# Attention in 64-key blocks on array tiles, even and odd tokens apart: one tuned kernel, one change of plan

## The chip, the cores and the metric

One core of one Trainium2 chip runs the whole program. The metric is the time on the device in microseconds (us); the median of several runs is quoted, with the lowest and highest. The engines are called PE (TensorE's matmuls), PEld (TensorE's weight loads, which overlap the matmuls), DVE (VectorE), ACT (ScalarE), POOL (GpSimd) and SP (SyncE, which issues transfers).

A *tile* below is one step of the attention: 112 query rows with the 16 rows of keys before them. A *row tile* is 128 rows of the residual stream, as the gMLP layers use it. The *tail* of a tile is everything after the attention proper: transpose o, multiply by `wo`, add the residual, normalise for the next layer.

## The reference, cut to what matters

There are four layers, attention, gMLP, attention, gMLP, each `x + f(layernorm(x))`, on 2048 tokens of 576 channels. The gMLP layers take about three quarters of the time and are untouched by the change. The attention has 32 heads of 18 channels; a token looks at 8 tokens, itself and every second one before it:

```python
W, dil = (8, 2)
off = jnp.arange(W) * dil
idx = pos[:, None] - off[None, :]          # tokens s, s-2, ..., s-14
...
logits = jnp.einsum('bhsd,bhswd->bhsw', q, kg) * scale
attn = _softmax(logits, axis=-1)
o = jnp.einsum('bhsw,bhswd->bhsd', attn, vg)
return o.transpose(...).reshape(B, S, D) @ wo
```

An even token sees only even tokens, an odd one only odd ones. A dense 128 x 112 block of logits, masked, is therefore at least half wasted, and the change goes after that.

## The kernel before: the parts that matter here

A tile is done in two half steps of 16 heads. Per half step there are 16 logits matmuls, one or two exponentials, one mask, 16 value products and one normalisation. o is transposed by a transfer on SP's queue. Filler matmuls (`JUNK`, two per half step, 128 rows x 512 columns, never read) run in the late steps.

```python
def JUNK(n):
    ...
        jt = self.PT_tile([P, 512], f32, "junk")
        for k_ in range(n):
            nc.tensor.matmul(jt[:, :], lhsT=wo_sb[:, k_ % 4, 0:P], rhs=wo_sb[:, (k_ + 1) % 4, 0:512],
                             start=True, stop=True)
...
def TAIL_A(t):                                   # half steps after the tile's last: 2
        nc.sync.dma_start_transpose(out=oT_t[:, :, :nq], in_=o_t[:nq, :])
        ...
def TAIL_B(t):                                   # 4: output product, residual, statistics
        ...
def TAIL_B2(t):                                  # 5: normalise, on POOL
        st["xn"] = self.ln_xn(x_new, st["nq"], mv, rstd, nmr, eng="pool")
...
ND0 = 3                                          # 3 of 5 channel groups projected before the first logits
...
for (off, fn) in ((2, TAIL_A(t)), (4, TAIL_B(t)), (5, TAIL_B2(t)), (6, TAIL_C(t))):
    s_ = plast + off
```

The normalisation is on POOL.

The softmax here doesn't subtract the row's maximum and nothing guards it: scores larger than these inputs give would overflow.

## Time and profile before

Before: 1348.4 us median (1346.5 to 1352.3, 4 runs beside the changed kernel; 1349.1 in the three first runs).

| stretch (profiled run) | us | how read |
|---|---|---|
| attention, layer 1 | 162.9 (25.2 to 188.1) | first projection matmul to first gMLP matmul |
| gMLP | 501.1 (188.1 to 689.2) | to the first projection of layer 2 |
| attention, layer 2 | 159.4 (689.2 to 848.6) | |
| gMLP and end | 499.8 (848.6 to 1348.4) | |
| first projection to first value product | 29.3 and 26.7 | layers 1 and 2 |
| late tile | 5.8 | value products of one tile to those of the next |

The head of the page: the second line gives each engine's busy time, share of the span and number of instructions; PEclk is TensorE's granted clock in tenths, over 40 equal slices.

```profile
span 1348.4 us, 21451 instructions
...
PE 1249.9 (93%) x8656; PEld 659.5 (49%) x8656; DVE 616.5 (46%) x1402; ACT 384.2 (28%) x595; POOL 356.4 (26%) x487
...
PEclk9999989999999999997999999899999999999999
```

The averages say nothing about the attention, which is a quarter of the span. The window table does. Columns: window, its length, then busy us and instruction count of each engine, the granted clock, the DMA engines' share, GB/s. These are the late steps of layer 1, and most of layer 2:

```profile
112.00:145.00 33.00, 30.22 (x497) 20.50 (x496) 29.63 (x74) 24.06 (x34) 20.88 (x14) 1.00 0.81 125
145.00:178.00 33.00, 29.48 (x498) 19.74 (x496) 29.75 (x77) 19.27 (x30) 18.29 (x13) 1.00 0.66 121
740.00:836.00 96.00, 87.93 (x1377) 57.37 (x1376) 81.70 (x196) 62.12 (x85) 53.02 (x36) 0.98 0.74 143
```

DVE is busy 29.7 of 33 us in the late steps and PE nearly as much, at full clock. In the timeline of one late tile (start, length, engine, line, operation):

```profile
808.18 1.19 SPq L568 DMA_TRANSPOSE oT_7002<-o_t_6993  x1
808.26 0.56 POOL L164 TENSOR_TENSOR ln_rstd<-ln_rstd,neg_half 112x1 f32<-112x1 f32 x1 [2.85 <-DVE ln_rstd L163]
808.92 2.29 POOL L181 TENSOR_SCALAR ln_xn_82<-x_new,ln_mv,ln_rstd 112x576 bf16<-112x576 f32 x1
...
809.50 1.40 PE L582 MATMUL pw<-wo_sb,oT_7004 128*128 128x288 bf16 x10
...
811.11 0.59 PE L517 MATMUL junk<-wo_sb 128*128 128x512 bf16 x2 [0.21 <-DVE v_ext L375]
```

The normalisation takes 2.29 us.

### The profile page before, as it was taken

How to read it: one execution, taken by the hardware profiler on the slowest of the kernel's cores; microseconds unless marked ns; L12 is line 12 of the kernel's file. 1: busy time of each engine (PE TensorE's matmuls, PEld its weight loads, DVE VectorE, ACT ScalarE, POOL GpSimd, SP SyncE). 2: the span in 40 equal slices, each digit the busy share in tenths (PEclk: the TensorE clock that was granted, in tenths of full speed). 3: DMA queues.
4: the chain of work that ended last, by engine and by line, in shares of the span. 5: the costliest groups of instructions: out<-in, count | busy, mean ns of one | idle time of the engine just before them, and what ended most of it. 6: DMA issues, size and time to landing. Idle time of an engine off the chain costs nothing.

```text
span 1348.4 us, 21451 instructions
## 1 busy us (share of the span) xinstructions
PE 1249.9 (93%) x8656; PEld 659.5 (49%) x8656; DVE 616.5 (46%) x1402; ACT 384.2 (28%) x595; POOL 356.4 (26%) x487
## 2 busy tenths in 40 slices
PE   1999969989999999998998987899999999999997
PEld 0456644434444444445754655444444444444576
DVE  4468858843322332332534878588323223333221
ACT  2556726620011111001126665465101111100000
POOL 7445547830000000002141646488000000000111
PEclk9999989999999999997999999899999999999999
DMA  9449759020000000009653677861100000000232
GB/s 264 98 94 145 121 134 214 1 90 6 9 10 9 10 9 9 0 4 266 179 137 62 151 145 129 181 125 41 43 9 9 10 9 9 2 7 1 72 113 67
DMA packets 180128, 101.04 MB, mean 75 GB/s; under 512 B 138276, under 2 KB 162212, under 8 KB 180028
## 3 DMA queue, kind: packets, MB, share of 16 engines
q1 hardware_dynamic: 170208, 84.15, 28.1%
q10 hardware_dynamic: 6364, 8.55, 2.2%
q0 software_dynamic: 3456, 6.96, 2.2%
q8 instruction: 68, 1.11, 0.3%
q14 instruction: 32, 0.26, 0.1%
HBM read 41.16 MB, written 16.52 MB: 43 GB/s over the span
## 4 chain that ended last, share of the span: by engine, by line
PE 62%; DVE 11%; POOL 10%; issue 7%; DMA 6%; ACT 3%; SPq 1%; ACTq 0%; POOLq 0%; DVEq 0%
PE pg L904 36%; PE po L941 9%; DVE z_junkD L819 4%; PE pp L412 3%; DMA QK<-stg 2%; POOL ln_xn_84 L181 2%; POOL ln_xn_81 L181 1%; POOL ln_rstd L164 1%; POOL z_rstd L835 1%; POOL ln_xn_83 L181 1%; POOL ln_xn_82 L181 1%; DMA wout_b<-in_B_w_out_dram 1%; DMA wv_sb<-in_A_wqkv_dram 1%; DMA win2b<-in_B_w_in_dram 1%; DVE z_msq L828 1%
## 5 line engine op out<-in xcount | busy, mean ns | idle before, releaser
L908 DVE TENSOR_TENSOR g_tmp<-pg,bsp 128x512 f32<-128x512 f32 x144 | 99.4, 692 | 435.5 <-PE pg L904 423.9
L412 PE MATMUL pp<-xnT,wqk_sb 128*128 128x512 bf16 x400 | 100.7, 394 | 29.8 <-DMA xnT<-ln_xn_84 28.5
L812 PEld LDWEIGHTS <-xnT 128*128 128x128 bf16 x800 | 78.4, 98 | 97.0 <-issue 13.0
L812 PE MATMUL pz<-win2a,xnT 128*128 128x512 bf16 x384 | 103.1, 379 | 5.9 <-ACT zp L816 4.4
L164 POOL TENSOR_TENSOR ln_rstd<-ln_rstd,neg_half 112x1 f32<-112x1 f32 (+2 forms) x70 | 43.4, 621 | 152.3 <-DVE ln_rstd L163 152.1
L812 PE MATMUL pz<-win2b,xnT 128*128 128x512 bf16 x256 | 77.0, 386 | 6.9 <-DMA win2b<-in_B_w_in_dram 6.9
L816 ACT ACTIVATE zp<-pz 128x1024 bf16<-128x1024 f32 x64 | 65.0, 1020 | 44.6 <-POOL z2b_9746 L845 18.9
L412 PEld LDWEIGHTS <-wqk_sb 128*128 128x128 bf16 x400 | 36.9, 100 | 71.2 <-issue 36.0
L819 DVE CUSTOM_DVE_ANT_0 z_junkD<-zp 128x1536 bf16<-128x1536 bf16 x32 | 56.9, 1777 | 18.7 <-ACT zp L816 18.7
L370 PE MATMUL pv<-wv_sb,xnT 128*128 128x288 bf16 (+1 forms) x380 | 62.2, 286 | 0.2 <-DVE stg L418 0.2
L76 POOL DMA_DIRECT2D wout_b<-in_B_w_out_dram x14 | 7.5, 541 | 172.4 <-PE pg L904 172.4
L76 POOL DMA_DIRECT2D QK<-stg x52 | 31.5, 608 | 73.0 <-ACT stg L420 28.0
L584 DVE TENSOR_TENSOR x_new<-pw,xo 112x288 f32<-112x288 f32 (+1 forms) x76 | 33.5, 445 | 18.0 <-PE pw L582 10.7
L420 ACT CAST stg<-pp 128x512 bf16<-128x512 f32 x54 | 31.0, 585 | 37.4 <-PE pp L412 22.7
L370 PEld LDWEIGHTS <-xnT 128*128 128x128 bf16 (+1 forms) x380 | 33.5, 97 | 15.8 <-issue 1.4
L489 PE MATMUL L_ps<-QK 18*128 18x112 bf16 (+1 forms) x1216 | 32.0, 210 | 4.9 <-DMA QK<-stg 1.7
L418 DVE CAST stg<-pp 128x512 bf16<-128x512 f32 x26 | 18.0, 691 | 37.0 <-PE pp L412 33.5
L159 DVE BATCH_NORM_STATS2 ln_st<-x_new 112x6 f32<-112x288 f32 (+1 forms) x76 | 33.9, 449 | 1.2
L489 PEld LDWEIGHTS <-QK 18*128 18x128 bf16 (+1 forms) x1216 | 20.4, 93 | 25.6 <-issue 21.6
L845 POOL TENSOR_SCALAR z2b_3101<-zp,z_rstd,z_nmr 128x256 bf16<-128x256 bf16 x16 | 32.4, 2024 | 0.0
L845 POOL TENSOR_SCALAR z2b_9746<-zp,z_rstd,z_nmr 128x256 bf16<-128x256 bf16 x16 | 32.4, 2023 | 0.0
L904 PE MATMUL pg<-W_sb,z2b_3093 128*128 128x512 bf16 x128 | 28.4, 379 | 1.9 <-DVE z2b_3093 L848 1.9
(549 smaller groups left out, 2513.3 us busy)
## 6 DMA issues: line engine op xcount, KB each, us to landing
xres_73<-x_new SPq DMA_DIRECT2D x18, 252.0 KB
xo<-xres_74 SPq DMA_DIRECT2D x18, 252.0 KB
xres_75<-x_new SPq DMA_DIRECT2D x18, 252.0 KB
QK<-stg POOLq DMA_DIRECT2D x52, 72.0 KB, 3.8
win2a<-in_B_w_in_dram SPq DMA_DIRECT2D x2, 1728.0 KB
QK<-stg SPq DMA_DIRECT2D x48, 72.0 KB
wqk_sb<-in_A_wqkv_dram ACTq DMA_DIRECT2D x4, 576.0 KB
out_dram<-ob SPq DMA_DIRECT2D x16, 144.0 KB
```

The source lines that it names most:

```text
L164: nc.gpsimd.tensor_tensor(out=rstd[:nrows, :], in0=rstd[:nrows, :], in1=self.neg_half[:nrows, :], op=ALU.pow)
L181: e.tensor_scalar(out=xn[:nrows, 0:D], in0=x_t[:nrows, :], scalar1=mv[:nrows, 0:1], scalar2=rstd[:nrows, 0:1], op0=ALU.subtract, op1=ALU.mult)
L370: nc.tensor.matmul(pv[:nk, 0:288], lhsT=self.xnT[:, c, QT * t:QT * t + nk], rhs=wv_sb[:, c, hh * 288:(hh + 1) * 288], start=(c == 0), stop ...
L412: nc.tensor.matmul(pp[:, :], lhsT=wqk_sb[:, c, wc0:wc0 + P], rhs=self.xnT[:, c, col0:col0 + 512], start=(c == 0), stop=(c == 4))
L489: nc.tensor.matmul(L_ps[:nk, j, ftl * QT:ftl * QT + nq], lhsT=kT[32 * j:32 * j + DH, g, QT * t:QT * t + nk], rhs=qT[32 * j:32 * j + DH, g, ...
L812: nc.tensor.matmul(pzvs[ci][:, sub * 512:sub * 512 + w], lhsT=self.xnT[:, c, PADL + i * P:PADL + (i + 1) * P], rhs=win2(c)[:, c0 + sub * 5 ...
L816: nc.scalar.activation(out=zp[:, c0:c0 + cn], in_=pzvs[ci][:, 0:cn], func=ACT.Gelu_apprx_tanh, accum_out=sums[:, ci:ci + 1])
L819: nc.vector.tensor_tensor_reduce(out=junkD[:], in0=zp[:, 0:SQ_D], in1=zp[:, 0:SQ_D], scale=1.0, scalar=0.0, op0=ALU.mult, op1=ALU.add, acc ...
L845: nc.gpsimd.tensor_scalar(out=z2b[b][:, i, :], in0=zp[:, b * 256:(b + 1) * 256], scalar1=rstd[:, 0:1], scalar2=nmr[:, 0:1], op0=ALU.mult, ...
L904: nc.tensor.matmul(pg[:, :], lhsT=z2b[jj][:, i, sub * P:(sub + 1) * P], rhs=W_sb[:, i, q * 512:(q + 1) * 512], start=(i == 0), stop=(i == ...
L908: nc.vector.tensor_tensor(out=tmp[:], in0=pg[:, :], in1=bsp[:, q * 512:(q + 1) * 512], op=ALU.add)
L941: nc.tensor.matmul(acc[hh], lhsT=uT[j // 2][:, j % 2, i * P:(i + 1) * P], rhs=wout_j(j)[:, hh * 288:(hh + 1) * 288], start=(j == 0), stop= ...
```

## The change

The intent is to relieve DVE. Even and odd tokens are kept apart (`QK[..., r, ...]`), so a tile needs two 64-key by 56-query blocks a head instead of one of 128 by 112: half the logits to exponentiate and mask. The blocks go to tiles of the PE array, two column halves for even and odd. All 32 heads are done in one step. o is transposed by TensorE against a permutation (which also puts the rows back in order). Tails work on 128 rows, 16 instead of 19 of them. Core of the diff:

```diff
-        def L_mm(s):                                  # 16 per half step
-                nc.tensor.matmul(L_ps[:nk, j, ftl * QT:ftl * QT + nq], lhsT=kT[...], rhs=qT[...],
-                                 start=True, stop=True, tile_position=(32 * j, 0))
+        def L_mm(t):                                  # 64 per tile
+                            nc.tensor.matmul(L_ps[64 * r:64 * r + nk, j, g * QH:g * QH + nq],
+                                             lhsT=QK[rows, g, 2 + r, k0:k0 + nk],
+                                             rhs=QK[rows, g, r, k0 + PADL // 2:k0 + PADL // 2 + nq],
+                                             start=True, stop=True, tile_position=(32 * j, 64 * r))
...
-        def JUNK(n):                                  # filler: gone
...
+        def OT(t):
+                tp = self.H_tile("tp")                # 12 matmuls against self.perm
+                nc.scalar.copy(out=oT[...], in_=tp[...])
...
-                nc.sync.dma_start_transpose(out=oT_t[:, :, :nq], in_=o_t[:nq, :])
...
-                st["xn"] = self.ln_xn(x_new, st["nq"], mv, rstd, nmr, eng="pool")
+                st["xn"] = self.ln_xn(x_new, P, mv, rstd, nmr, eng="act")
...
-        for d in range(ND0):                          # 3 of 5 groups, then logits
-            for cc in cb_ccs(0):
+        for cc in range(2):                           # all 5 groups, all heads
+            for d in range(ND):
+                pro.append((4 * cc + 3, PG(d, cc)))
...
-            for (off, fn) in ((2, TAIL_A(t)), (4, TAIL_B(t)), (5, TAIL_B2(t)), (6, TAIL_C(t))):
+            post.append((t + 2, 0, OT(t)))
+            post += [(t + 1, 3, TAIL_A(u)), (t + 2, 1, TAIL_B(u)), (t + 3, 2, TAIL_B2(u)), (t + 3, 4, TAIL_C(u))]
```

V, projections, value products, transposed o and output product (`pv`, `pp`, `O_ps`, `tp`, `pw`) now all take turns in two PSUM buffers (`H_tile`), where the kernel before had three small ones and one for the value products.

## The prediction

> **What bounds the kernel now.** By the window table, the 1348 us span holds two attention layers (0 to 188 us, 689 to 851 us); the rest are gMLP layers (PE about 97% busy), which the change leaves alone.
>
> - Prologue: 60 q/k projection matmuls before the first logits (46.5 and 704 us in the tile view of L_ps).
> - Early steps, with the other 140 projection matmuls: PE-bound (30.2 of 32 us in 80:112, 29.2 of 30 us in 740:770).
> - Late steps: a 112-row tile takes about 5.8 us (the chain of waits repeats so). DVE is fullest, 59.4 of 66 us in 112:178. Per tile it runs two masks of 1.09 us, two reciprocals of 0.25, two normalisations of 0.46, two residual adds and two statistics of 0.45. PE has slack: junk matmuls fill it, and the timeline shows it waiting for DVE.
>
> **What the change removes and adds, per tile.**
>
> DVE: even and odd tokens apart halve the masked logits, so one mask replaces two; reciprocal, normalisation and residual add are merged; 16 tails replace 19. My sum falls from 5.9 to about 3.9 us. POOL's 2.29 us normalisations go to ACT (0.87 us). ACT: exponentials halve from 3.7 to 1.84 us, but v and oT copies and the normalisation bring it back to about 4.1 us. Neither should bind.
>
> PE: the trace gives start-to-start 12 to 13 ns for a four-row-tile logits matmul, 25 ns for a value product, 122 ns for N=288. Before: logits 0.66 us with mode switches, PV 0.8, V 1.23, output 1.23, junk 0.86: 4.8 us. After: logits and value products double in number, 32 to 64 each, on 64-column tiles. The Trainium skill (TensorEngine Tiling (Array Packing), Tile-to-Partition Mapping, Restrictions) says column tiling disables Fast Weight Load; and (Tiling Modes, Key Properties) that changing mode drains TensorE, which shows here as about 0.1 us. I estimate 13 ns a matmul with four tiles in flight: logits 0.85, PV 0.85, V 1.25, oT 0.5, output 1.23, more switches 0.6: about 5.3 us. So the late bound moves from DVE (5.8) to PE (5.3 to 5.8).
>
> The prologue needs all 100 first-half projection matmuls (216 ns each) before the first logits: 8.6 us later, work taken out of the early steps. In the second attention layer this start is exposed, with the QK transfers behind it; in the first it overlaps the layernorm ramp. The tail loses its transpose DMA (PE waits 4 us for it at 178.7 us): about -3 us a layer.
>
> **Sum.** First attention layer about -10 us, second about -5 us. Tuned orders usually recover a little more: **1332 us**, range 1290 to 1368. Faster by over 2%: 0.38; within 2%: 0.46; slower: 0.16.
>
> **What would show it right or wrong.** First logits near 50 and 715 us; the gMLP stretch unchanged (about 501 us); late tile period 5.0 to 5.8 us, PE fullest, DVE near 65%; logits and PV about 0.9 us each per tile in the timeline; no oT wait before the gMLP layer.
>
> **What would make it wrong.** First, the small-tile rate. At 7 ns a matmul the tile costs 4.5 us and the kernel about 1310; at 25 ns (weight loads of column tiles not overlapping) PE costs 6.8 us a tile and the kernel about 1380. Second, V, projections, PV, oT and output now share two PSUM buffers (before, three plus one), so PE may wait for ACT's in-order queue; it would show as PE waits released by ACT copies of v_ext, stg or oT. Third, the QK transfers, two thirds on POOL's queue, may delay the first logits.

## The result, and the profile after

After: 1433.9 us median (1430.2 to 1437.3, 4 runs), against 1348.4. Ratio 1.063 (95% interval 1.059 to 1.067): slower by over 6%. (A ratio here is the mean time of one kernel's runs over the mean of the other's of the same rounds, so not quite the ratio of the medians quoted.) The result is correct.

| stretch (profiled runs) | before | after | difference |
|---|---|---|---|
| attention, layer 1 | 162.9 | 207.1 | +44.2 |
| gMLP | 501.1 | 500.0 | -1.1 |
| attention, layer 2 | 159.4 | 197.7 | +38.3 |
| gMLP and end | 499.8 | 500.7 | +0.9 |
| first projection to first value product | 29.3, 26.7 | 46.5, 42.9 | +17.2, +16.2 |
| late tile | 5.8 | 7.8 to 9.2 | |

The loss is in the attention layers alone. It is not in the late tiles alone: by the first value products of tiles 0, 9 and 18, of the 44.2 and 38.3 us the start takes 17.2 and 16.2, the next nine tiles, with projections among them, 17.0 and 9.7, and the last nine 10.7 and 13.1. (7.8 to 9.2 us is the usual length of a late tile; one step a layer has no output product, and around it and at the layer's end they are shorter.) The page's head after:

```profile
span 1431.1 us, 27266 instructions
...
PE 1292.7 (90%) x11735; PEld 699.0 (49%) x11840; DVE 557.9 (39%) x1198; ACT 368.7 (26%) x563; POOL 292.5 (20%) x462
...
PEclk9988767999999999998999976599999999999998
```

Two things are visible. DVE, ACT and POOL all became *less* busy, as intended, and the span is longer. And PEclk dips to 5, 6 and 7 exactly in the slices of the attention. Windows of the late tiles of both layers:

```profile
135.00:165.00 30.00, 25.62 (x642) 17.59 (x639) 12.04 (x25) 13.07 (x18) 6.20 (x11) 0.66 0.30 73
165.00:195.00 30.00, 23.56 (x616) 17.38 (x616) 13.39 (x27) 14.67 (x20) 4.68 (x6) 0.76 0.24 64
870.00:900.00 30.00, 24.17 (x591) 16.85 (x591) 12.00 (x25) 12.96 (x17) 5.88 (x8) 0.66 0.31 88
```

Neither DVE, ACT nor POOL is half busy. PE is busy for 79 to 85% of the time, but at two thirds to three quarters of the clock. So nothing is full at full clock, and the tile takes half as long again. This suggests a ring: a chain of work in which each step waits for the one before, and which closes on itself. The chain of waits (start, length, what) shows one:

```profile
878.69 1.04 POOL ln_rstd L177
...
879.82 0.27 POOL ln_nmr L181
...
880.12 0.87 ACT ln_xn L190
880.99 0.61 ACT oT L484
...
881.64 3.07 PE pw L505 x12
...
884.74 0.77 DVE x_new L507
...
885.53 0.82 DVE ln_st L172 x2
...
886.68 0.72 DVE o_t L467
...
887.61 1.33 POOL ln_rstd L177
...
889.33 0.87 ACT ln_xn L190
890.19 0.61 ACT oT L484
...
890.85 3.08 PE pw L505 x12
```

From one `pw` to the next are 9.21 us. The output product of row tile u feeds DVE's residual and statistics (with the attention's own `o_t` between them in DVE's queue), then POOL's reciprocal root, then ACT's normalisation `ln_xn`. Behind `ln_xn`, in ACT's queue, stands the copy of oT. That copy has nothing to do with `ln_xn`: its own input, the transposing product, was done at 889.12 us, and yet the copy started at 890.19, when `ln_xn` ended. The next output product needs the copy. So row tile u + 1 cannot start its output product until row tile u has been normalised. Nothing in the mathematics asks for this. Nor can it be read off the code: there `OT` of step t + 3 is emitted before `TAIL_B2` of the same step, and the trace has them the other way round.

In the groups of instructions, the last columns are the idle time before the group and what ended most of it:

```profile
L505 PE MATMUL pw<-wo_sb,oT 96*128 96x288 bf16 x384 | 77.0, 371 | 36.2 <-ACT oT L484 36.2
L438 ACT ACTIVATE P_sb<-L_ps 128x896 bf16<-128x896 f32 (+1 forms) x76 | 63.7, 887 | 88.4 <-PE O_ps L458 78.6
```

PE waited 36.2 us for ACT's copy; ACT in turn waited 78.6 us for PE's value products, which stand behind `pw` in PE's queue and must be done before a P buffer is written again. The two queues hold each other up. Also, `pw` takes 3.07 us at a granted clock of 0.50 (window 881.7 to 884.6 us); the same twelve matmuls take 1.64 us at full clock. So the 9.21 us are not the ring alone. TensorE was busy for 7.5 us of them, much of that because its clock was low, and waited 1.73 us.

### The profile page after: what moved, and what is told of

It is laid out like the page before. It is cut to its first block, busy times and chain, and to the rows that moved or that the text cites. A ratio compares the mean times of both kernels' runs of the same rounds, so it can differ in the third digit from the quotient of the medians.

```text
span 1431.1 us, 27266 instructions
## 1 busy us (share of the span) xinstructions
PE 1292.7 (90%) x11735; PEld 699.0 (49%) x11840; DVE 557.9 (39%) x1198; ACT 368.7 (26%) x563; POOL 292.5 (20%) x462
## 5 line engine op out<-in xcount | busy, mean ns | idle before, releaser
L803 PE MATMUL pg<-W_sb,z2b 128*128 128x512 bf16 x2254 | 501.0, 379 | 4.5 <-DVE z2b L747 1.9
L803 PEld LDWEIGHTS <-z2b 128*128 128x128 bf16 x2304 | 225.3, 98 | 273.7 <-DVE z2b L747 2.4
L798 ACT ACTIVATE z1T<-pz 128x1024 bf16<-128x1024 f32 x72 | 73.7, 1023 | 556.8 <-PE pz L795 526.6
L795 PE MATMUL pz<-xnT,w 128*128 128x512 bf16 x710 | 163.3, 382 | 3.7 <-DMA w<-in_B_w_in_dram 3.2
L840 PEld LDWEIGHTS <-uT 128*128 128x128 bf16 x1152 | 114.3, 99 | 44.1 <-issue 12.0
L840 PE MATMUL po<-wout_b,uT 128*128 128x288 bf16 x864 | 116.0, 291 | 10.6 <-DMA wout_b<-in_B_w_out_dram 10.5
L795 PEld LDWEIGHTS <-w 128*128 128x128 bf16 x720 | 70.5, 98 | 90.6 <-DMA w<-in_B_w_in_dram 5.1
L505 PE MATMUL pw<-wo_sb,oT 96*128 96x288 bf16 x384 | 77.0, 371 | 36.2 <-ACT oT L484 36.2
L808 DVE TENSOR_TENSOR uT<-g_tmp,z1T 128x512 bf16<-128x512 f32 x144 | 99.5, 692 | 16.0 <-ACT z1T L798 6.0
L744 POOL TENSOR_SCALAR z2b<-zp,z_rstd,z_nmr 128x256 bf16<-128x256 bf16 x96 | 102.4, 1076 | 3.9 <-POOL z_nmr L736 0.9
L438 ACT ACTIVATE P_sb<-L_ps 128x896 bf16<-128x896 f32 (+1 forms) x76 | 63.7, 887 | 88.4 <-PE O_ps L458 78.6
```

Of the source, the lines that this page charges most:

```text
L505: nc.tensor.matmul(pw[:, hh, 0:288], lhsT=oT[:, c, P * u:P * u + P], rhs=wo_sb[0:96, c, hh * 288:(hh + 1) * 288], start=(c == 0), stop=(c ...
L744: nc.gpsimd.tensor_scalar(out=z2b[b][:, i, :], in0=zp[:, b * 256:(b + 1) * 256], scalar1=rstd[:, 0:1], scalar2=nmr[:, 0:1], op0=ALU.mult, ...
L795: nc.tensor.matmul(pz1[:, qq, :], lhsT=w1[:, c, sub * P:(sub + 1) * P], rhs=self.xnT[:, c, PADL + (q2 + qq) * 512:PADL + (q2 + qq + 1) * 512],
L798: nc.scalar.activation(out=z1T[:, q2 * 512:(q2 + nq2) * 512], in_=pz1[:, 0:nq2, :].rearrange("p a b -> p (a b)"), func=ACT.Gelu_apprx_tanh)
L803: nc.tensor.matmul(pg[:, :], lhsT=z2b[jj][:, i, sub * P:(sub + 1) * P], rhs=W_sb[:, i, q * 512:(q + 1) * 512], start=(i == 0), stop=(i == ...
L808: nc.vector.tensor_tensor(out=u[:, sub, q * 512:(q + 1) * 512], in0=tmp[:], in1=z1T[:, q * 512:(q + 1) * 512], op=ALU.mult)
```

## The experiments

Three theories, not exclusive, were on the table:

- **O**, the order of ACT's queue makes the ring.
- **C**, the clock: dropping the filler let TensorE's clock fall, and everything else follows from that.
- **P or Q**, the start: the first value product comes 17 us later in each layer, because of the projections' staging buffers (P) or of the transfers of QK (Q).

All ratios are to the kernel before, of the same rounds. The rounds ran on four chips; the median of the kernel before was 1347.3 to 1349.2 us in all of them, so plain times of different rounds compare to within a few us. The expectations use the letters a little differently: "theory Q" in x2, x3 and x4 is O here, and so is "rival R" in y2; "rival S" is that column-tiled matmuls are too slow.

### x1_stg5: a fifth staging buffer

```diff
-        NVB = 6
+        NVB = 4
-  stg_tiles[(d, cb)] = sb.tile([P, 4, CBW // 2], bf16, name="stg", tag="stg", bufs=4)
+  stg_tiles[(d, cb)] = sb.tile([P, 4, CBW // 2], bf16, name="stg", tag="stg", bufs=5)
```

(Two V buffers were given up to make room.)

> The changed kernel with five staging tiles for the projections in place of four (and four v tiles in place of six, to make room). Theory P: in the prologue five head groups are open at once but only four staging tiles exist, so the fifth group's copy out of PSUM waits for a QK transfer and holds one of the two PSUM buffers; PE then runs the second five groups single-buffered (3.5 us a group in place of 2.2). Expected: first value product of the second attention layer 6 to 10 us earlier after its first projection (43 us now), 12 to 20 us off the whole kernel, about 1417 us. Rival (QK transfers set the start): nothing changes, within 4 us of 1434.

Measured: 1433.8 us (1431.8 to 1434.9), ratio 1.064, unchanged. In layer 2 fifty projections ran back to back in 10.96 us, and yet the first value product came 43.2 us after the first projection (42.9 in the changed kernel). In the table of waits (total, times, longest) the logits now wait 16.7 us for the transfers, where they waited 3.5 us in the changed kernel (first line):

```profile
PE L_ps L427 <- DMA QK<-stg: 3.5, 4, 1.5
PE L_ps L427 <- DMA QK<-stg: 16.7, 13, 3.6
```

Theory P falls: faster projections only moved the wait to the transfers. This leaves the transfers, when they can begin and how long their queues need; y3 tests it.

### x2_xn_after_exp: normalise behind the next exponentials

```diff
-  (t + 3, 2, TAIL_B2(u)), (t + 3, 4, TAIL_C(u))
+  (t + 5, 2, TAIL_B2(u)), (t + 5, 4, TAIL_C(u))
...
+                with tc.issue_after(last_exp[0].ins):
                     st["xn"] = self.ln_xn(x_new, P, mv, rstd, nmr, eng="act")
```

> The changed kernel; the layernorm write of a tail stays on ACT but stands in ACT's queue behind the next step's exponentials, not ahead of the oT copy. Theory Q (order of ACT's queue): one tail's residual add, statistics, rstd and layernorm write stand in a ring with the next tail's output matmuls, 8 to 9 us a tile. Without it the late tile period falls from 8.9 to 6 to 7 us and the kernel by 45 to 70 us, to 1365 to 1390. Rival C (clock: removed junk matmuls and half-rate TensorE set the late period): the period stays above 8 us, clock about 0.66, kernel above 1415. Rival S (column-tiled matmuls too slow): the same as C, nothing changes.

Measured: 1402.7 us (1395.9 to 1405.1), ratio 1.039 (1.036 to 1.042): 31 us won by moving one 0.87 us instruction, emitted two steps later and behind the exponentials. The copy of oT now waits for its own input alone (layer 2; the last figure is ACT's idle time before it):

```profile
859.04 0.71 ACT L486 CAST oT<-tp 96x672 bf16<-96x672 f32 x1 [1.18 <-PE tp L483]
```

Late tiles took 6.5 us in layer 1 where the clock was full, but still 9.2 in parts of layer 2. There `pw` again took 3.06 us: at the low clock a tile is as long without this ring as with it. It was less than I expected, and the output product still waits for ACT's copy:

```profile
PE pw L507 <- ACT oT L486: 28.5, 32, 1.3
```

### x3_xn_pool: normalise on POOL, as the kernel before did

```diff
-  st["ln"] = (x_new,) + tuple(self.ln_stats(sb, x_new, P, want_nmr=True))
+  st["ln"] = (x_new,) + tuple(self.ln_stats(sb, x_new, P, want_nmr=False))
-  st["xn"] = self.ln_xn(x_new, P, mv, rstd, nmr, eng="act")
+  st["xn"] = self.ln_xn(x_new, P, mv, rstd, nmr, eng="pool")
```

> The changed kernel with the tails' layernorm write back on POOL (2.3 us there against 0.87 on ACT). Theory Q: as good as the reordered one, 1365 to 1390, although the write itself is slower, because it is out of the ring. Rival (ACT is overloaded): better than the reordered one by over 10 us. Rival C or S: above 1415.

Measured: 1401.6 us (1397.5 to 1404.8), ratio 1.040. This takes 0.87 us a tile off ACT, which x2 does not, and gives the same time. So it is not ACT's load; it is what stands behind what in its queue. PE still waited 25.2 us (31 times) for oT.

### x4_before_nojunk: the kernel before, without its filler

```diff
-    def __init__(self, ..., njunk=2, ...):
+    def __init__(self, ..., njunk=0, ...):
```

> The kernel before with its junk matmuls taken out. Theory Q says that PE has slack there, so this costs little: 1345 to 1362, and the clock drops only in part of the late steps. Rival C says that the junk matmuls hold the clock: granted clock near 0.66 in the late steps (112 to 178 us, 770 to 836 us) and 1375 or more.

Measured: 1375.5 us (1374.9 to 1380.4), ratio 1.021 (1.019 to 1.024). I expected nearly nothing; it is 28 us (against 1347.3 in the same rounds). The windows 112 to 178 us and 770 to 836 us had clock 1.00 or close to it in the kernel before; now:

```profile
112.00:178.00 66.00, 50.66 (x802) 32.57 (x801) 49.95 (x128) 38.22 (x55) 35.11 (x23) 0.87 0.53 114
770.00:836.00 66.00, 52.08 (x786) 33.95 (x785) 47.62 (x121) 36.34 (x52) 36.57 (x25) 0.87 0.67 141
```

So the filler in the kernel before was paid work, and removing it is a plausible second cause (theory C). PE's wait for the transposed o also rose, to 40.5 us in all, from about 10: the lower clock does not act alone even here.

### y2_junk: small filler in the changed kernel

```diff
                 pv = self.H_tile("pv")
+                if t >= 10:
+                    for k_ in range(8):
+                        nc.tensor.matmul(pv[:, k_ % 2, 288:512], lhsT=wo_sb[0:96, k_ % 4, 0:P],
+                                         rhs=wo_sb[0:96, (k_ + 1) % 4, 0:224], start=True, stop=True)
```

> The changed kernel with 8 filler matmuls of 224 columns added before each V product (from tile 10 on), into PSUM columns that nothing reads; the queue order is left as it is. Removing the old filler from the kernel before cost it 28 us. Theory C (the change lost its clock with the filler, and at half clock its own matmuls are longer: output product 3.07 us against 1.64): granted clock over the late tiles rises from about 0.66 to above 0.9, 15 to 30 us are won, result 1404 to 1419. Rival R (the ring through ScalarE's queue sets the period and the low clock is only its consequence): late tiles stay at 8 us or more, result 1425 to 1440 although the clock rises.

Measured: 1443.4 us (1438.1 to 1448.5), ratio 1.071: worse than without filler. The clock fell in layer 1 and rose a little in layer 2 (0.76 and 0.85 over the attention, against 0.80 and 0.80), late tiles took 8 to 11 us, PE waited 31.8 us for oT. The time is the rival's, or a little over it, but the clock was not raised as theory C needs, so y2 does not test it.

### y3_dmajor: the start

```diff
-        for cc in range(2):
-            for d in range(ND):
+        for d in range(ND):
+            for cc in range(2):
                 pro.append((4 * cc + 3, PG(d, cc)))
-            if cc == 0:
-                pro.append((3, VW(0)))
-                pro.append((3, VW(1)))
+        pro.append((3, VW(0)))
+        pro.append((3, VW(1)))
```

The transfers of a channel group can begin when both its halves (`cc`) are projected. In the changed kernel this is after the sixth projection group of ten; here it is after the second.

> The changed kernel with the ten projections of the first 1024 tokens ordered so that both halves of a channel group follow each other, so that the QK transfers of the first group can start after two projections and not after six. Theory Q (the row transfers of QK, not the projections, set the first logits): first projection to first PV falls from 43 us to about 35 us in each layer, result 1412 to 1424. Rival P (transfers are not what the start waits for, or the queues need the same time whenever they begin): under 5 us won, result 1428 to 1436.

Measured: 1418.3 us (1413.8 to 1419.7), ratio 1.051 (1.048 to 1.055): 15.6 us under the changed kernel. First projection to first value product fell from 46.5 and 42.9 us to 39.7 and 36.2. The transfers did begin earlier: in layer 2, 18.8 us after the first projection in the changed kernel (first pair of lines; first projection at 732.7 us), 6.4 us in y3 (second pair; 723.3 us). The first line of a pair is from the view of tile QK, with first and last start:

```profile
L78 SPq DMA_DIRECT2D QK<-stg x14: 786/787/891, 751.5 to 789.4; - x14
775.59 1.03 PE L458 MATMUL O_ps<-v_ext,P_sb 64*64 64x19 bf16 x64 [0.43 <-DVE P_sb L445]
...
L78 SPq DMA_DIRECT2D QK<-stg x13: 786/787/962, 729.7 to 755.8; - x13
759.49 1.03 PE L458 MATMUL O_ps<-v_ext,P_sb 64*64 64x19 bf16 x64 [0.37 <-DVE P_sb L445]
```

Theory Q holds, and the start is a cause of its own. It is still 10 us above the kernel before in each layer.

### y4_tail_later: the output product one step later

```diff
-  (t + 2, 1, TAIL_B(u)), (t + 3, 2, TAIL_B2(u)), (t + 3, 4, TAIL_C(u))
+  (t + 3, 1, TAIL_B(u)), (t + 6, 2, TAIL_B2(u)), (t + 6, 4, TAIL_C(u))
```

with `ln_xn` behind the exponentials as in x2.

> The order of x2_xn_after_exp, and the output product of a row tile emitted one step later too, so that it reads a transposed o that was copied a whole tile earlier. Theory O (after x2, the output product still waits 0.8 us each for ScalarE's copy of oT, 28 us in all, and this is on the ring): the wait of PE for that copy nearly goes, late tiles fall from 6.5 us to about 5.7, result 1375 to 1392. Rival C (the clock or VectorE sets the tile by then, the wait only moves to another instruction): 1396 to 1406, and the wait shows up at logits, PV or the transposing product.

Measured: 1372.8 us (1367.9 to 1376.2), ratio 1.018 (1.014 to 1.022), but the **result is wrong** (relative error 0.27). By the code, five normalised row tiles wait for their transposition at the layer's end, and the ring of buffers for them has four, so one is overwritten. No part of the argument needs the wrong values, and a1 below repeats the order mended. The time is 61 us under the changed kernel, 30 of them beyond x2. Late tiles took 5.6 us in most of layer 2, and the wait is all but gone:

```profile
PE pw L507 <- ACT oT L486: 4.3, 4, 1.3
```

And nobody touched the clock, yet it rose from 0.80 and 0.80 over the two attention layers to 0.91 and 0.96 (the windows below; the changed kernel's stand under b3). The profiled run is the fastest of the four, but in all four the clock over the whole span was 0.961 to 0.975, against 0.926 to 0.933.

```profile
26.00:203.70 177.70, 147.81 (x3420) 97.00 (x3434) 83.16 (x172) 81.65 (x107) 57.30 (x90) 0.91 0.45 91
701.50:865.80 164.30, 138.32 (x3417) 92.13 (x3433) 77.52 (x145) 78.18 (x102) 46.76 (x83) 0.96 0.46 104
```

So the low clock of the changed kernel is in good part a *consequence* of the order. Most of what y4 won came that way: both layers together are 62.8 us shorter than in the changed kernel, and of these PE's busy time gave 43.7, for the same matmuls and so by the clock, and its idle time 19.1. The early tiles gained as well: the first nine took 70.7 and 65.9 us, against 87.1 and 78.7 in the changed kernel and 70.1 and 69.0 in the kernel before.

### z2_all: everything at once

The order of y4, the projections of y3, four filler matmuls of y2 a tile, and

```diff
-  eng=(nc.sync if dma_rr[0] % 3 == 0 else nc.gpsimd)
+  eng=((nc.sync, nc.gpsimd, nc.scalar)[dma_rr[0] % 3] if cb == 0 else ...)
```

> All together: the order of y4_tail_later, projections ordered as in y3_dmajor, the first half's QK transfers over three queues instead of two, and 4 filler matmuls a tile. If the causes add: 31 for the order, 10 to 20 for the start, 10 to 25 for the clock and the second wait, so 1345 to 1375, about the time of the kernel before. If they overlap (clock and order are two sides of the same loss), 1375 to 1395.

Measured: 1369.8 us (1364.7 to 1377.8), ratio 1.015, the same wrong values as y4. Only 3 us under y4, although y3 alone had won 15.6. The first value product came 44.1 and 41.7 us after the first projection, so the gain at the start was given back. The filler cannot have done it, as it begins at tile 10. That leaves the third queue, which is ACT's own: a1 below has the same order and projections without it, and starts after 40.4 and 36.2 us. Neither was kept.

### a1_best: the order and the start, mended

```diff
+            s_b = t + 3 if t + 3 <= NT - 1 else t + 2
+            s_c = min(t + 6, NT - 1 if u < NS - 4 else max(NT, s_b + 1))
-            post += [..., (t + 3, 1, TAIL_B(u)), (t + 6, 2, TAIL_B2(u)), (t + 6, 4, TAIL_C(u))]
+            post += [..., (s_b, 1, TAIL_B(u)), (s_c, 2, TAIL_B2(u)), (s_c, 4, TAIL_C(u))]
```

(against y4; plus y3's projections)

> y4_tail_later mended (its result was wrong because five normalized row tiles waited for their transposition at the layer's end and the ring has four buffers; now only the last four are put off), with the projections ordered as in y3_dmajor and the last row tiles not put off further than needed. If the queue order and the start are separate causes, the 15 us that y3 won come off the 1373 of y4: 1352 to 1362, and correct. If they overlap (the start wins nothing once the tiles are short): 1366 to 1376.

Measured: 1363.0 us (1359.4 to 1367.2), ratio 1.011 (1.008 to 1.014), correct. It is 1 us outside the range of the theory that the two causes are separate, and well under that of the rival. The late tiles of layer 1, from the timeline of PE:

```profile
160.33 0.70 PE L427 MATMUL L_ps<-QK 18*64 18x56 bf16 x64
160.96 0.51 PE L483 MATMUL tp<-perm,o_t 56*96 56x112 bf16 x11
161.40 1.64 PE L507 MATMUL pw<-wo_sb,oT 96*128 96x288 bf16 x12
162.98 0.68 PE L460 MATMUL O_ps<-v_ext,P_sb 64*64 64x19 bf16 x64
163.90 1.42 PE L366 MATMUL pv<-wv_sb,xnT 128*64 128x288 bf16 x20 [0.24 <-DVE x_new L509]
165.80 0.25 PE L483 MATMUL tp<-perm,o_t 56*96 56x112 bf16 x1 [0.49 <-DVE ln_rstd L176]
165.98 0.70 PE L427 MATMUL L_ps<-QK 18*64 18x56 bf16 x64
...
167.03 1.64 PE L507 MATMUL pw<-wo_sb,oT 96*128 96x288 bf16 x12
```

From `pw` to `pw` are 5.63 us. The parts are 0.70 + 0.25 + 0.51 + 1.64 + 0.68 + 1.42 = 5.2 us of TensorE work, of which 0.3 us overlap from one part to the next, and two waits of 0.24 and 0.49. So this is the tile filled by TensorE that the prediction had foreseen, at the length foreseen, once the order allows it and while the clock is full. In layer 2 it was not always full, and tiles took up to 8.5 us. From 800 to 830 us PE was busy nearly all the time and yet at 0.63 (third number from the end):

```profile
800.00:830.00 30.00, 29.02 (x760) 21.23 (x756) 15.24 (x33) 15.95 (x21) 4.57 (x6) 0.63 0.33 85
```

So breaking the ring does not by itself keep the clock up; what pulled it down here was not found.

### a2_best_junk4, b1_best_full2: filler on top of the best version

a2 adds y2's filler, four a tile. b1 adds two a tile of the old size:

```diff
+                if t >= 10:
+                    for k_ in range(2):
+                        nc.tensor.matmul(pv[:, k_ % 2, :], lhsT=wqk_sb[:, k_ % 4, 0:P],
+                                         rhs=wqk_sb[:, (k_ + 1) % 4, 0:512], start=True, stop=True)
```

> a1_best with 4 filler matmuls of 224 columns a tile from tile 10 on. If the clock still costs time when the ring through ScalarE is gone (y4 ran its last tiles of layer 1 at 0.77): 3 to 10 us under a1_best. If the filler now stands in the way on a TensorE that sets the tile (4 x 0.1 us x 2 x 9 tiles = 7 us): 3 to 10 us over a1_best.

> a1_best with 2 full-size filler matmuls (128 rows x 512 columns, the size of the old filler) a tile from tile 10 on, where a2 had 4 of 96 rows x 224 columns; about 0.43 us of TensorE a tile in both. If the size of the filler is what holds the clock: granted clock of both attention stages 0.94 or more, 1350 to 1360. If filler of any size does not matter once the ring is short: clock as in a2 (0.89 to 0.91), 1362 to 1372.

Measured: a2 1368.3 us (1359.4 to 1370.1), ratio 1.013 (1.010 to 1.017). b1 1365.8 us (1355.7 to 1371.4, 5 runs), ratio 1.015 (1.012 to 1.017). Neither differs from a1 (1.008 to 1.014) beyond the intervals. Over its five runs b1's time goes with its mean clock over the whole span: 1355.7 us at 0.976, 1361.3 at 0.968, 1365.8 at 0.963, 1369.3 at 0.962, 1371.4 at 0.958. The profiled run was the first of these, so its clock in the attention (0.93 and 0.96) is not typical. What is left to the clock varies by some 15 us from run to run, in the same kernel; both expectations about the clock are therefore inconclusive.

### b3_after_full4: full-size filler in the changed kernel

b1's edit with `range(4)` for `range(2)`, made to the changed kernel and nothing else. This is the test of theory C that y2 could not give, because y2 did not raise the clock.

> The changed kernel with 4 full-size filler matmuls (128 rows x 512 columns) a tile from tile 10 on; nothing else. y2 had 8 of 96 rows x 224 columns and stayed at 0.65 in the late tiles of layer 1, at 1443 us. If size is what counts: late clock above 0.9, output product back to 1.64 us, 1395 to 1420. If the ring keeps the clock down whatever the filler: clock below 0.8 in the late tiles, 1425 to 1450.

Measured: 1437.0 us (1433.7 to 1443.9), ratio 1.066. Windows over the two attention layers (clock is the third number from the end), first of the changed kernel, then of b3 (rounded; over b3's exact stretches, 25.9 to 237.2 and 737.1 to 934.2 us, the clock is 0.85 and 0.90):

```profile
25.60:232.70 207.10, 166.97 (x3419) 105.45 (x3433) 83.42 (x173) 82.97 (x108) 60.03 (x92) 0.80 0.34 79
732.70:930.40 197.70, 162.86 (x3417) 104.09 (x3433) 78.09 (x146) 80.07 (x103) 49.37 (x85) 0.80 0.33 87
```

```profile
25.00:232.00 207.00, 164.26 (x3422) 100.59 (x3444) 81.49 (x169) 82.17 (x106) 60.13 (x91) 0.86 0.34 79
732.00:930.00 198.00, 157.86 (x3469) 98.83 (x3491) 78.66 (x148) 79.30 (x103) 49.33 (x85) 0.91 0.35 88
```

The clock rose to about 0.86 and 0.91, and nothing was won. In the late windows (135 to 225 and 840 to 920 us) it was 0.67 to 0.89, which fits neither expectation; the time is the ring's. PE's wait for oT was hardly shorter than the 36.2 us of the changed kernel, once for each row tile of the two layers, so the wait did not go when the clock rose:

```profile
PE pw L509 <- ACT oT L488: 35.5, 32, 2.2
```

The filler costs PE time of its own (22.7 us busy in the recorded ones), so the clock's worth is not measured cleanly here; what is shown is that as long as the ring stands, buying clock with this filler does not pay. Small filler (y2) raised the clock in one layer of two and full-size filler in both, in part; what exactly the clock follows stays open.

### a3_pool: the best version with the normalisation on POOL

```diff
-  st["xn"] = self.ln_xn(x_new, P, mv, rstd, nmr, eng="act")      # behind the exponentials
+  st["xn"] = self.ln_xn(x_new, P, mv, rstd, nmr, eng="pool")
-  s_c = min(t + 6, NT - 1 if u < NS - 4 else max(NT, s_b + 1))
+  s_c = min(t + 4, NT - 1 if u < NS - 4 else max(NT, s_b + 1))
```

> a1_best with ln_xn moved to GpSimd instead of put behind the exponentials on ScalarE, one step later than in the changed kernel; the output product one step later as in a1_best. If only the order of ScalarE's queue matters: the same as a1_best within 8 us, as x3 was the same as x2. If ScalarE's load (57% busy in the late tiles of y4) is the next limit: 10 or more under a1_best.

Measured: 1373.7 us (1371.9 to 1374.9), ratio 1.019 (1.017 to 1.021). That is 11 us over a1, a result that neither expectation allowed. In the profile two tiles at the end of the projections took 10.7 and 9.2 us in layer 1 (5.9 and 7.4 in a1); why is open. So leaving `ln_xn` on ACT, as the change has it, is not the mistake. Its place in the queue is (x2). a3 changes the engine and, against a1, the step of emission at once, so its 11 us are put down to neither.

## Why the prediction was wrong, point by point

I predicted 1332 us (1290 to 1368), with the weight on no change or faster. It came to 1434.

- **The step that failed: "ACT ... back to about 4.1 us. Neither should bind."** As a load this was right: ACT is busy 12.96 of 30 us in a late window of the changed kernel. But ACT bound by *order*. Its copy of oT stood behind a normalisation that waited for POOL, DVE and the previous output product. x2 and x3, two different ways of getting the normalisation out of the copy's way, won 31 and 32 us. Moving the output product a step away from the copy won 30 more (y4). Together that is 61 of the 85 us, part of them by way of the clock, as said under y4. The prediction's second doubt named the right sign to look for, PE waits released by ACT's copies of oT, and gave it no size: it went into a sum of loads as zero. A sum of loads cannot contain a ring. (That doubt also blamed the two shared PSUM buffers. No run changed their number, so their part is open; the order alone was enough for the 61 us.)
- **"The prologue needs all 100 first-half projection matmuls ...: 8.6 us later."** Mis-sized, because the start does not end with the first logits. These came 9.0 and 9.6 us later after the first projection, close to the forecast, but in layer 2 they were 4 of a tile's 64 (at 757.2 us); 48 of them followed only at 770.5 us. The first value product came 17.2 and 16.2 us later. x1 showed that faster projections don't help, and y3 that the transfers had to wait for the sixth of ten groups. Starting them earlier won 15.6 us. This was the prediction's third doubt. Nor did the early steps get shorter for the work taken out: the first nine tiles took 17.0 and 9.7 us longer, and with the order mended (y4) about as long as before. In the first layer the delay is not hidden by the layernorm ramp as I wrote; it is as long as in the second.
- **"PE has slack: junk matmuls fill it."** Wrong about the kernel before: its filler is worth 28 us (x4). For the changed kernel I then over-corrected and suspected the missing filler. y4 raised the clock without any, and b3 put filler in and won nothing. The granted clock over the attention fell from 0.96 and 0.97 to 0.80 and 0.80, and is back at 0.90 and 0.84 in a1. It makes every tile longer (`pw` 3.07 us against 1.64), but PE's wait does not come from it alone: b3 raised the clock and the wait stayed.
- **The small-tile rate** was the first doubt, and there the prediction was right: 64 logits matmuls take 0.70 us, 64 value products 0.68 us (0.85 predicted for each). V took 1.42 (1.25), oT 0.76 (0.5), output 1.64 (1.23). The parts add up to 5.2 us a tile against 5.3, which is luck in part: the errors cancel, and 0.6 us for mode switches were in the forecast that are not a part of the measured sum.
- **"The late bound moves from DVE (5.8) to PE (5.3 to 5.8)"** was wrong for the changed kernel (7.8 to 9.2) and right for a1 at full clock (5.6). DVE was to be near 65% busy in the late tiles and was 40 to 45%, the tiles being longer. DVE's work did fall, from 220.1 to 161.5 us over both attention layers in the window table.
- **"gMLP stretch unchanged (about 501 us)"**: 500.0. Right.
- **"The tail loses its transpose DMA: about -3 us a layer"**: not seen. The last value products to the first gMLP matmul took 9.5 and 9.7 us before and 10.1 and 10.1 after.

What is left between a1 and the kernel before is about 15 us. By stretches, a1's attention takes 170.3 and 171.2 us against 162.9 and 159.4. (Its profiled run was the slowest of its four.) The first value product is 11.1 and 9.5 us later than before, which is as much as all of it. The tiles after it took 2.7 us less than before in layer 1 and 3.4 more in layer 2, where the clock was low. By the code, the later start follows from the plan of the change: a step needs all heads, so it must wait for all projections and transfers, while the kernel before starts with half the heads. The late tiles are hardly shorter than before (5.6 against 5.8), so there is little to pay this back with. No version here beats the kernel before.

## What to carry to other kernels

When a change moves work between engines, write down each in-order queue as a list, per step, and ask of every entry what the entries *behind* it are waiting for; a cheap instruction with a late input, in front of a cheap one that an early consumer needs, can close a ring that no table of busy time shows. Take the order from the trace, not from the code. When all engines are half idle and a period is constant, look in the chain of waits for a loop and break it by distance (one more step between producer and consumer) before taking away load. A low granted clock can be the symptom of such a loop: mend the order first, then judge the filler.

## What the Trainium skill lacked or had wrong

- *TensorE: Matmul & The Clock Gate*, under "Wait — 56ns, not 53.3ns?", says that start-to-start never drops below about 25 ns, however small N is. With several array tiles in flight, 64 logits matmuls of 56 columns took 0.70 us and 64 value products of 19 columns 0.68 us, about 11 ns each. The floor does not hold for matmuls that go to different tiles. That section does not say so, though Part 3 of the page, on packing small matmuls, lets tiles start much closer together.
- *TensorEngine Tiling (Array Packing)*, Restrictions, says that column tiling disables Fast Weight Load. No cost of it stands out at these sizes: the 11 ns above include the weight loads, one for each matmul. No run has the fast load on to compare with.
- *TensorE: Matmul & The Clock Gate*, "HAM oscillation — how this bites in real kernels", gives as the abstract rule no PE-idle gaps over about 3.4 us. In the changed kernel's late tiles (135 to 220 and 840 to 915 us) no gap between recorded matmuls is longer than 2.1 us, and the clock is 0.66 in several windows there. The idle times are of the kind of the page's "A second HAM failure mode: psum-queue depth-cycling", where frequent short idle times are enough; that they are the reason here is not shown, as a1 had 0.63 over 30 us in which PE was busy for 29.0. The rule alone would have called this kernel safe.
- The same page has no figure for how much filler, or of what size, holds the clock. Here two of 128 rows x 512 columns a half step were worth 28 us in the kernel before; eight of 96 rows x 224 columns a tile gave the changed kernel a clock of 0.76 and 0.85 against 0.80 and 0.80, and four of full size about 0.86 and 0.91.
- *TensorE: Matmul & The Clock Gate* says that the queues of ScalarE and VectorE are strict FIFO. No page draws from it what cost most here: that an instruction with a late input delays unrelated ones behind it in the same engine's queue. Moving one 0.87 us normalisation was worth 31 us (x2), part of them by way of the clock.
